# A feed-forward layer's last six chunks: the up-projection as a block product of seven, with its weight sums made on the way

## The chip, the cores and the metric

The kernel runs on one core of a Trainium2 chip. The core has a matrix engine (TensorE, PE in the profile; its weight loads are PEld), a vector engine (VectorE, DVE), an activation engine (ScalarE, ACT), a general engine (GpSimd, POOL) and a queue engine that here only issues transfers (SyncE, SP). Each engine runs its own instructions in order and waits on semaphores for the others. SBUF is the on-chip memory of 128 partitions; PSUM holds the results of matmuls. The metric is the device time of one launch in microseconds; the median of three runs is compared.

## The reference

An attention layer with a window feeds a gated feed-forward layer (FFN). In short:

```python
batch, n_heads, seq, head_dim = (8, 8, 576, 64)
scores = scale * np.matmul(q, k.transpose(0, 1, 3, 2))
mask = (rel >= 0) & (rel < window)                    # window 128
scores = np.where(mask, scores + bias[None], -1000000000.0)
attn = np.exp(scores - max); attn = attn / (sum + 1e-09)
attn_out = np.matmul(attn, v)
x = attn_out.transpose(0, 2, 1, 3).reshape(4608, 512)
h = x @ w_in                                          # 512 -> 2048
g = h * (1.0 / (1.0 + np.exp(-1.702 * h)))
out = g @ w_out                                       # 2048 -> 512
```

All of it is float32. The matmuls run in a shorter float format (fp32r), so every large operand is cut in a high part and a rest, and a product of two operands is made of three: high by high, rest by high, high by rest.

## The kernel before

**FFN.** The 4608 tokens are 18 chunks of 256. `Job` walks the 16 blocks of 128 hidden features of one chunk; a block of a chunk is a step, 288 in all. A step's *up* (L552) is 12 matmuls of 128x256 into `h_ps`: three products (`xh` by both parts of `w`, `xl` by the high part) over four slices of the 512 inputs. Then ACT makes tanh (L557), DVE the gelu product `g` (L558, which reads PSUM), ACT casts `g` to `gh` (L561), and POOL makes the rest `gl = g - gh` (L562). The step's *down* (L571) is 6 matmuls of 128x512 into the two accumulators of the chunk. Up of the next step is issued before down of this one. At a chunk's start `split_x` cuts `x` (casts L536 on DVE or ACT, subtractions L538 on DVE and POOL by turns); at its end DVE scales the accumulators into `o` (L587) and ACT's queue writes them out.

**Weights.** `w_in` and `w_out` come as 16 + 16 blocks of 512 KB over SP's queue and are decoded at the start: L212 and L213 on DVE, casts on ACT, the rest on POOL (L217). All 32 stay in SBUF, under the tags `w1_0` to `w1_15` and `w2_0` to `w2_15`.

**Attention.** It is cut in units, one for a pair of heads and one or two blocks of 128 queries. A call of `tick()` moves a pipeline of units by one stage: cuts of q, k, v (L292 to L312), scores (L334), bias and minimum (L362), exponentials (L381), normalising (L406), transposes (L442), the cut of the transposed probabilities (L461), the product with v (L499), and the sums into `x` (L520 to L529). There are 144 units; the first two batches have a simpler path without cuts.

**What sets the order.** The program interleaves FFN steps and ticks. `due` says for each batch how many units must be done by which chunk and from which chunk on they may start; the loop spreads the ticks by that. A scheduler then orders the instructions of each engine; queues are in order after that. `in_turn` adds dependencies between matmuls to keep their order. `XBUFS = 4` buffers hold chunks of `x` that attention has begun.

Of the kernel before, what the change touches and what calls it, by code (L numbers as in the profile page):

```python
# [8 lines left out]
F32 = mybir.dt.float32  # L9
F32R = mybir.dt.float32r  # L10
# [14 lines left out]
NF = DFF // P  # L25
NC = DM // P
T = 256
NCH = NT // T
XBUFS = 4
WINDOW = 128  # L30
MASKED = -1.0e38
SCALE = 0.125
# [4 lines left out]
WB = 2  # L37
# [105 lines left out]
def tile_kernel(ctx: ExitStack, tc: tile.TileContext, q0, k0, v0, qT, kT, v, w_in, w_out, out):  # L143
    nc = tc.nc

    const = ctx.enter_context(tc.tile_pool(name="const", bufs=1))
    raw = ctx.enter_context(tc.tile_pool(name="raw", bufs=3))
    att = ctx.enter_context(tc.tile_pool(name="att", bufs=2))
    xp = ctx.enter_context(tc.tile_pool(name="xp", bufs=1))
    ffn = ctx.enter_context(tc.tile_pool(name="ffn", bufs=2))  # L150
    ps = ctx.enter_context(tc.tile_pool(name="ps", bufs=1, space=PSUM))

    def move(dst, src):

# [333 lines left out]
    def mix(u):  # L488
# [4 lines left out]
        for c in u.chunks:  # L493
# [22 lines left out]
    def sum_up(u, g):
        hp = u.pair % NP
# [14 lines left out]
    def split_x(c, x):  # L532
        xh = xp.tile([P, NC, T], F32R, name="xh")
        xl = xp.tile([P, NC, T], F32R, name="xl")
        for k in range(NC):
            (nc.scalar.copy if c in BESIDE else nc.vector.tensor_copy)(xh[:, k], x[:, k])  # L536
            sub = nc.vector if k % 2 else nc.gpsimd
            sub.tensor_tensor(xl[:, k], x[:, k], xh[:, k].bitcast(F32), ALU.subtract)  # L538
        return xh, xl

    class Job:


        def __init__(self, c, f0, f1, begun=None):
            self.c, self.f0, self.f1, self.begun = c, f0, f1, begun
            self.gs = {}

        def up(self, f):
            h = ps.tile([P, T], F32, name="h_ps", bufs=2)
            ops = [(z, x, k) for z, x in ((0, self.xh), (1, self.xh), (0, self.xl)) for k in range(NC)]  # L550
            for n, (z, x, k) in enumerate(ops):
                nc.tensor.matmul(  # L552
                    h, w1[f][:, z, k * P:(k + 1) * P], x[:, k],
                    start=(n == 0), stop=(n == len(ops) - 1))

            g = ffn.tile([P, T], F32, name="g")
            nc.scalar.activation(g, h, AF.Tanh, scale=0.851)  # L557
            nc.vector.scalar_tensor_tensor(g, g, 1.0, h, ALU.add, ALU.mult)  # L558
            gh = ffn.tile([P, T], F32R, name="gh")
            gl = ffn.tile([P, T], F32R, name="gl")  # L560
            nc.scalar.copy(gh, g)  # L561
            nc.gpsimd.tensor_tensor(gl, g, gh.bitcast(F32), ALU.subtract)  # L562
            self.gs[f] = (gh, gl)

        def down(self, f):
            if f == self.f0:
                self.acc = [ps.tile([P, DM], F32, name=f"acc{t}") for t in range(T // P)]
            gh, gl = self.gs.pop(f)
            for n, (g, z) in enumerate(((gh, 0), (gh, 1), (gl, 0))):
                for t, acc in enumerate(self.acc):  # L570
                    nc.tensor.matmul(  # L571
                        acc, g[:, t * P:(t + 1) * P], w2[f][:, z],
                        start=(f == self.f0 and n == 0), stop=(f == self.f1 - 1 and n == 2))

        def finish(self):
            if self.f1 < NF:
                self.sum = xp.tile([P, T // P, DM], F32, name="xf", tag="xf", bufs=XBUFS)
# [3 lines left out]
            o = xp.tile([P, T // P, DM], F32, name="o", tag="x0")  # L581
            for t, acc in enumerate(self.acc):
                if self.begun:
                    nc.vector.tensor_tensor(o[:, t], acc, self.begun.sum[:, t], ALU.add)
                    nc.vector.tensor_scalar(o[:, t], o[:, t], 0.5, None, ALU.mult)
                else:
                    nc.vector.tensor_scalar(o[:, t], acc, 0.5, None, ALU.mult)  # L587
                at = self.c * T + t * P
                nc.scalar.dma_start(out[at:at + P, :], o[:, t])
# [17 lines left out]
    ticks = 0  # L607

    def tick():

        nonlocal ticks
        n = ticks

        def stage(k, *steps):
            u = units[n + k] if 0 <= n + k < len(units) else None
            for step in steps:
                if u:
                    step(u)

        stage(1, split_q)  # L620
        stage(-2, flip, split_v)
        stage(0, load_v)
        stage(-1, biased)
        stage(1, split_rest)
        stage(-1, exponents)
        stage(-1, normal)
        stage(-2, high, low)
        stage(0, scores)
        stage(-3, mix)
        if n + 1 < len(units) and units[n + 1] and loads:  # L630
# [38 lines left out]

    jobs = [Job(0, 0, F0), Job(1, 0, NF)]  # L670
    jobs.append(Job(0, F0, NF, jobs[0]))
    jobs += [Job(c, 0, NF) for c in range(2, NCH)]
# [10 lines left out]
    def begin(j):  # L683
        j.xh, j.xl = split_x(j.c, xf.pop(j.c, first_x))
        j.up(j.f0)

    begin(jobs[0])
    seen = 0
    flat = [(j, f) for j in jobs for f in range(j.f0, j.f1)]
    for now, (j, f) in enumerate(flat):  # L690

        if halves < 2 * NF:
            owed += max(
                (2 * g + 2 - halves - owed) / max(need[g] - DECODE_AHEAD - now, 1)
                for g in range(halves // 2, NF))
            while owed >= 1 and halves < 2 * NF:
                owed -= 1
                fetch_upto(halves // 2 + 1 + FETCH_AHEAD)
                decode_next()

        pace, last = 0.0, 0
        for n, by, start in due:
            if start > seen:
                break
            last = n + 3
            pace = max(pace, (n + 3 - ticks - credit) / max(starts[by] - 1 - SLACK - now, 1))
        credit += pace
        while credit >= 1 and ticks < last:
            credit -= 1
            tick()  # L710
        if now + 1 < len(flat):
            nj, nf = flat[now + 1]
            if nj is j:
                j.up(nf)
            else:
                begin(nj)
                seen = max(seen, nj.c)
        j.down(f)
        if f == j.f1 - 1:
            j.finish()  # L720


def build(nc, arrays):
# [50 lines left out]
```

## Time and profile before

| | |
|---|---|
| median of 3 runs | 1065.19 us (1064.08 to 1066.76) |
| profiled execution | 1068.36 us, span 1066.3 us, granted clock 0.995 |
| PE busy | 1052.9 us, 99% of the span |
| DVE, ACT, POOL busy | 660.5, 597.2, 603.5 us (62, 56, 57%) |
| up matmuls, L552 | 3456 of 128x256 |
| down matmuls, L571 | 1728 of 128x512 |
| transfers | 78.45 MB, mean 74 GB/s |

The page lists busy time by engine, the span in forty slices, the chain of waits that ended last, and groups of instructions. Other views used below are stretches (busy time of each engine between two times), one line's instructions, the chain in order of time, and the timeline. A line number such as L552 is that of the kernel before; the change's own lines are numbered by the changed kernel.

### The profile page before, as it was taken

What the parts mean: (1) busy time and instruction counts of PE and PEld (TensorE: products, weight loads), DVE (VectorE), ACT (ScalarE), POOL (GpSimd) and SP (SyncE); (2) the same over time, 40 slices, a digit from 0 to 9 for tenths busy, and PEclk for the clock granted to TensorE, in tenths of its full rate; (3) what the DMA queues carried; (4) which work ended last, traced back from release to release, by engine and by line L of the source; (5) the groups of instructions that cost most, each with busy time, mean ns of one, the idle gap of its engine ahead of it and who ended that gap; (6) DMA issues with size and microseconds to landing.
All of it is one profiled execution on the core that took longest, in us unless ns stands there. A gap on an engine that the chain in (4) does not pass through costs nothing.

```text
span 1066.3 us, 21362 instructions
## 1 busy us (share of the span) xinstructions
PE 1052.9 (99%) x7041; PEld 929.1 (87%) x7041; DVE 660.5 (62%) x2117; ACT 597.2 (56%) x1811; POOL 603.5 (57%) x863
## 2 busy tenths in 40 slices
PE   9899999999999999999999999999999999999998
PEld 5567787889989999999999999999999999998987
DVE  6797522568887777545767668767877687313121
ACT  6879853466666565535555556655665656322222
POOL 4579933567676666554656557656666665323232
PEclk9899999999999999999999999999999999999999
DMA  8872001223222132102121223212222221000000
GB/s 307 281 261 73 25 22 56 73 67 96 75 76 81 51 102 67 57 14 71 54 79 52 71 62 91 66 60 78 79 63 85 57 78 28 20 2 20 1 21 20
DMA packets 88109, 78.45 MB, mean 74 GB/s; under 512 B 36800, under 2 KB 79296, under 8 KB 88000
## 3 DMA queue, kind: packets, MB, share of 16 engines
q1 hardware_dynamic: 82240, 67.14, 21.4%
q10 hardware_dynamic: 5760, 9.96, 2.6%
q8 instruction: 55, 0.90, 0.3%
q14 instruction: 54, 0.44, 0.1%
HBM read 67.63 MB, written 9.44 MB: 72 GB/s over the span
## 4 chain that ended last, share of the span: by engine, by line
PE 94%; DVE 3%; ACT 1%; DMA 1%; issue 1%; POOL 0%; SPq 0%; DVEq 0%; POOLq 0%; ACTq 0%
PE h_ps L552 38%; PE acc L571 37%; PE s_ps L334 5%; PE x_ps L499 5%; PE t_ps L442 4%; PE x_ps L476 2%; PE t_ps L419 1%; PE sb_ps L324 1%; PE s_ps L324 1%; DVE wc L213 1%; DMA rw<-w_out 1%; ACT pb L374 1%; DVE rec L392 0%; PE acc L189 0%; DVE rw L212 0%
## 5 line engine op out<-in xcount | busy, mean ns | idle before, releaser
L562 POOL TENSOR_TENSOR gl<-g,gh 128x256 fp32r<-128x256 f32 x288 | 218.0, 757 | 292.2 <-ACT gh L561 224.9
L552 PE MATMUL h_ps<-xh,w 128*128 128x256 f32 x2304 | 370.2, 284 | 1.1 <-POOL w L217 0.6
L552 PEld LDWEIGHTS h_ps<-xh,w 128*128 128x128 f32 x2304 | 328.5, 189 | 34.5 <-issue 2.8
L571 PE MATMUL acc<-w,gh 128*128 128x512 f32 x1152 | 324.9, 400 | 0.0
L558 DVE SCALAR_TENSOR_TENSOR g<-g,h_ps 128x256 f32<-128x256 f32 x288 | 119.6, 415 | 207.9 <-ACT g L557 206.5
L557 ACT ACTIVATE g<-h_ps 128x256 f32<-128x256 f32 x288 | 110.4, 383 | 229.4 <-PE h_ps L552 207.3
L571 PEld LDWEIGHTS acc<-w,gh 128*128 128x128 f32 x1152 | 196.5, 189 | 27.9 <-ACT g L557 0.3
L552 PE MATMUL h_ps<-xl,w 128*128 128x256 f32 x1152 | 194.6, 280 | 0.0
L561 ACT CAST gh<-g 128x256 fp32r<-128x256 f32 x288 | 116.9, 406 | 129.5 <-DVE g L558 121.1
L571 PE MATMUL acc<-w,gl 128*128 128x512 f32 x576 | 188.0, 401 | 0.0
L552 PEld LDWEIGHTS h_ps<-xl,w 128*128 128x128 f32 x1152 | 164.2, 188 | 6.0
L312 POOL TENSOR_TENSOR K<-rk,K 128x384 fp32r<-128x384 f32 (+1 forms) x120 | 109.0, 909 | 65.2 <-ACT Q L292 15.9
L381 ACT ACTIVATE pb<-pb,mins 128x256 f32<-128x256 f32 (+2 forms) x216 | 104.9, 487 | 43.8 <-DVE mins L362 40.1
L571 PEld LDWEIGHTS acc<-w,gl 128*128 128x128 f32 x576 | 92.6, 188 | 9.5 <-issue 0.9
L311 POOL TENSOR_TENSOR Q<-rq,Q 64x256 fp32r<-64x256 f32 (+1 forms) x120 | 83.1, 692 | 22.2 <-DVE K L310 4.9
L406 DVE TENSOR_SCALAR pb<-pb,rec 128x256 f32<-128x256 f32 (+2 forms) x216 | 91.8, 461 | 3.2
L362 DVE CUSTOM_DVE_ANT_0 pb<-s_ps,bias 128x256 f32<-128x256 f32 (+3 forms) x240 | 85.7, 377 | 4.1 <-PE s_ps L334 2.8
L392 DVE TENSOR_SCALAR rec<-sums 128x2 f32<-128x2 f32 (+3 forms) x144 | 48.5, 336 | 58.4 <-ACT pb L381 53.6
L334 PE MATMUL s_ps<-K,Q 128*128 128x256 f32 (+1 forms) x432 | 79.8, 289 | 0.4 <-DVE mins L362 0.4
L310 DVE CAST K<-rk 128x384 fp32r<-128x384 f32 (+1 forms) x120 | 52.5, 438 | 41.2 <-PE s_ps L334 34.2
L461 DVE TENSOR_TENSOR pl<-t_ps,ph 128x512 fp32r<-128x512 f32 (+2 forms) x120 | 72.2, 604 | 9.3 <-ACT ph L455 6.6
L442 PE MATMUL t_ps<-ident,pb 128*128 128x128 f32 x408 | 74.2, 272 | 0.0
(68 smaller groups left out, 1322.2 us busy)
## 6 DMA issues: line engine op xcount, KB each, us to landing
rk<-kT SPq DMA_DIRECT2D x72, 192.0 KB, 2.5
rq<-qT SPq DMA_DIRECT2D x96, 128.0 KB, 2.3
out<-o ACTq DMA_DIRECT2D x36, 256.0 KB, 2.1
rw<-w_in SPq DMA_DIRECT2D x16, 512.0 KB, 6.5
rw<-w_out SPq DMA_DIRECT2D x16, 512.0 KB, 7.0
rk<-kT SPq DMA_DIRECT2D x48, 128.0 KB, 2.2
rv<-v SPq DMA_DIRECT2D x96, 64.0 KB, 1.9
rq<-q SPq DMA_DIRECT2D x16, 128.0 KB, 2.6
```

What stands on the lines that cost most here:

```text
L312: nc.gpsimd.tensor_tensor(K2, rk, K1.bitcast(F32), ALU.subtract)
L334: nc.tensor.matmul(u.s[:b.rows, e, b.first:b.end], u.Q[:, b.q0 - u.q0:b.q0 - u.q0 + b.rows], k[:, ko:ko + b.end - b.first], start=(z == 0) ...
L362: nc.vector.tensor_tensor_reduce(b.p[ra:rb, cs:b.end], u.s[ra:rb, e, cs:b.end], bias[head][ra:rb, cs:b.end], -SCALE, BIG, ALU.add, ALU.min ...
L381: nc.scalar.activation(live, live, AF.Exp, bias=u.mins[:b.rows, e:e + 1], scale=-1.0, accum_out=u.sums[:b.rows, e:e + 1],)
L406: nc.vector.tensor_scalar(live, live, u.rec[:rows, e:e + 1], None, ALU.mult)
L442: nc.tensor.transpose(u.t[:c.n, w:w + b.rows], b.p[:b.rows, col:col + c.n], ident[:b.rows, :b.rows])
L552: nc.tensor.matmul(h, w1[f][:, z, k * P:(k + 1) * P], x[:, k], start=(n == 0), stop=(n == len(ops) - 1))
L557: nc.scalar.activation(g, h, AF.Tanh, scale=0.851)
L558: nc.vector.scalar_tensor_tensor(g, g, 1.0, h, ALU.add, ALU.mult)
L561: nc.scalar.copy(gh, g)
L562: nc.gpsimd.tensor_tensor(gl, g, gh.bitcast(F32), ALU.subtract)
L571: nc.tensor.matmul(acc, g[:, t * P:(t + 1) * P], w2[f][:, z], start=(f == self.f0 and n == 0), stop=(f == self.f1 - 1 and n == 2))
```

## The change

The classical way, a step at a time, stays for chunks 0 to 11 (`S0 = 12`). The last six chunks are taken in three pairs. For a pair, the 512 inputs are halved, the two chunks are the two columns, and two feature blocks are the two rows of a 2x2 block product in Winograd's form of Strassen's scheme: seven products in place of eight. Block `j` of eight covers features `2j` and `2j + 1`. Each product is 6 matmuls of 128x256 (two slices of inputs, three part products). The first two, B11 and B21, belong to the plain operands; X and Y are two PSUM buffers in which sums grow over several products, and copies by ACT and additions by DVE make the four results from them. The weight operands are A11, A12, A22 and four sums S1 to S4; the token operands are B11, B21, B22 and four combinations T1 to T4.

The weight sums are made by `sums(j)` in the last 20 classical steps (`SUMS`), one block every two steps: six DVE operations on SBUF, then for two pairs of sums a cast by ACT, a subtraction by POOL. All seven operands, cut in two parts, go to DRAM (`part`) over SP's queue, and `factor` reads them back in a ring of five buffers of 512 KB, two operands a buffer; the buffers are those of the first weight matrix, which is needed no more. `Pair.split` cuts the seven token operands. `linked` pins TensorE's order through the whole block product: each product is followed by a `cover` of downs of the block before. The last two classical downs (`COVER = 2`) are kept for the first pair's start.

So that the last steps are free of attention, batches 2 to 7 may all start once chunk 2 is begun, and all attention is due 20 steps before the block product. Chunks of `x` that are done too early are sent to DRAM (`send`) and recalled one chunk ahead (`recall`). `XBUFS` becomes 5; `o` uses the buffers of another pool.

```diff
-XBUFS = 4
+XBUFS = 5
+S0 = 12
+T2 = 2 * T
+COLS = 2 * P
+RING = 5
+SUMS = 20
+COVER = 2
+ORDER = "A11", "A12", "S2", "S3", "S1", "S4", "A22"
+OPERANDS = "B11", "B21", "T2", "T3", "T1", "B22", "T4"
...
+    def send(ct):
+        away[ct] = dram.tile([P, NC, T], F32, name=f"x{ct}")
+        nc.sync.dma_start(away[ct], xf.pop(ct))
+    def recall(ct):
+        if ct in away:
+            nc.sync.dma_start(home(ct), away.pop(ct))
...
+    def sums(j):
+        f, g = w1[2 * j], w1[2 * j + 1]
+        for name, src in (("A11", f[:, :, :COLS]), ("A12", f[:, :, COLS:]), ("A22", g[:, :, COLS:])):
+            nc.sync.dma_start(part(j, name), src.bitcast(F32))
+        a = att.tile([P, 2 * COLS], F32, name="sa", tag="ph")
+        b = att.tile([P, 2 * COLS], F32, name="sb", tag="pl")
+        nc.vector.tensor_tensor(a, g[:, 0].bitcast(F32), g[:, 1].bitcast(F32), ALU.add)
+        nc.vector.tensor_tensor(b, f[:, 0].bitcast(F32), f[:, 1].bitcast(F32), ALU.add)
+        nc.vector.tensor_tensor(a[:, COLS:], a[:, :COLS], a[:, COLS:], ALU.add)
+        nc.vector.tensor_tensor(a[:, :COLS], b[:, :COLS], a[:, :COLS], ALU.subtract)
+        nc.vector.tensor_tensor(b[:, :COLS], a[:, COLS:], b[:, :COLS], ALU.subtract)
+        nc.vector.tensor_tensor(b[:, COLS:], b[:, COLS:], b[:, :COLS], ALU.subtract)
+        for s, names in ((a, ("S3", "S1")), (b, ("S2", "S4"))):
+            st = xp.tile([P, 2, 2 * COLS], F32R, name="st", tag="xf", bufs=XBUFS)
+            nc.scalar.copy(st[:, 0], s)
+            nc.gpsimd.tensor_tensor(st[:, 1], s, st[:, 0].bitcast(F32), ALU.subtract)
+            for i, name in enumerate(names):
+                nc.sync.dma_start(part(j, name), st[:, :, i * COLS:(i + 1) * COLS].bitcast(F32))
...
+    def factor(n):
+        at, side = divmod(n, 2)
+        while len(ring) < min(at + RING, (NCH - S0) // 2 * len(parts)):
+            r = const.tile([P, 2, 2, COLS], F32R, name="ring", tag=f"w1_{len(OPERANDS) + len(ring) % RING}")
+            nc.sync.dma_start(r.bitcast(F32), parts[len(ring) % len(parts)])
...
+        def product(self, j, n, bank, start):
+            w, x = factor(self.first + j * len(ORDER) + n), self.x[OPERANDS[n]]
+            ops = [(z, y, k) for z, y in ((0, 0), (1, 0), (0, 1)) for k in range(2)]
+            linked([
+                nc.tensor.matmul(
+                    bank, w[:, z, k * P:(k + 1) * P], x[:, y, k],
+                    start=start and i == 0, stop=i == len(ops) - 1, skip_group_check=True)
+                for i, (z, y, k) in enumerate(ops)])
...
     units, due = [], []
     for b in range(B):
-        start = max((b * S + S - 1) // T - XBUFS, 0)
         if b < WB:
...
-                due.append((len(units), (b * S + lo) // T, start))
+                due.append((len(units), (b * S + lo) // T, 0))
         else:
             units += whole_batch(b)
-            due.append((len(units), b * S // T, start))
+            due.append((len(units), b * S // T, WB))
...
+    for c in range(S0, NCH):
+        starts[c] = steps - SUMS
...
+        if made < NF // 2 and now >= len(flat) - SUMS + 2 * made:
+            sums(made)
+            made += 1
```

**TensorE in the last chunks.** Before, around the start of the last chunk; `h_ps` is an up, `acc` a down:

```order
L552 MATMUL h_ps<-xh,w_1_525 128x256 x3
L552 MATMUL h_ps<-xl,w_1_525 128x256 x4
L552 MATMUL h_ps<-xh,w_2_573 128x256 x8
L552 MATMUL h_ps<-xl,w_2_573 128x256 x4
L571 MATMUL acc_14643<-w_0_455,gh 128x512 x2
L571 MATMUL acc_14643<-w_0_455,gl 128x512
```

After, from the second block to the third of the first pair; `X_ps` and `Y_ps` take products (`xB`, `xT` are token operands, `ring` the weight operands), `accs` are downs with `gs`:

```order
L693 MATMUL X_ps<-xB_13093,ring 128x256 x6
L693 MATMUL Y_ps<-xB_13096,ring 128x256 x6
L752 MATMUL accs<-w_0_485,gs 128x512 x6
L693 MATMUL X_ps<-xT_13105,ring 128x256 x6
L752 MATMUL accs<-w_0_485,gs 128x512 x6
L693 MATMUL Y_ps<-xT_13108,ring 128x256 x6
L693 MATMUL X_ps<-xT_13111,ring 128x256 x6
L752 MATMUL accs<-w_1_592,gs 128x512 x6
L693 MATMUL X_ps<-xB_13100,ring 128x256 x6
L693 MATMUL Y_ps<-xT_13115,ring 128x256 x6
L752 MATMUL accs<-w_1_592,gs 128x512 x6
```

Seven products of six and four groups of six downs make a block of two features for two chunks. At the very start of the first pair there are only two groups of late classical downs between the first products, and the others stand one behind the other.

**VectorE in the last classical steps.** Before, in steps 178 to 180, the operations of attention stand between the gelu products (L558):

```order
L558 SCALAR_TENSOR_TENSOR g<-g,h_ps 128x256
L310 CAST K_10795<-rk 128x384
L362 ISA pb,mins<-s_ps,bias_75 128x256
L362 ISA mins 128x1
L526 TENSOR_TENSOR carry<-x_ps,xb 64x128
L529 TENSOR_TENSOR xf<-x_ps,xb 64x128
L529 TENSOR_TENSOR xf<-x_ps,xb 64x256
L461 TENSOR_TENSOR pl<-t_ps,ph 128x512
```

After, there is no attention left; between the gelu products (L576) stand the sums (L626 to L631) and the first pair's token operands (L675 to L686):

```order
L576 SCALAR_TENSOR_TENSOR g<-g,h_ps 128x256
L631 TENSOR_TENSOR sb<-sb 128x256
L626 TENSOR_TENSOR sa<-w_9_1113 128x512
L628 TENSOR_TENSOR sa<-sa 128x256
L679 TENSOR_TENSOR xf<-xf 128x512
L576 SCALAR_TENSOR_TENSOR g<-g,h_ps 128x256
L681 TENSOR_TENSOR xf<-xf 128x512
L627 TENSOR_TENSOR sb<-w_8_1043 128x512
L629 TENSOR_TENSOR sa<-sb,sa 128x256
```

The sums of all eight blocks lie between the gelu products of steps 174 and 187; the 16 subtractions that belong to them (L635) lie in POOL's order among the `gl` of the same steps.

**SyncE at the start.** Before, the loads of early units and weights follow one another:

```order
L155 DMA VV<-v 128x3x128
L155 DMA rq<-q 128x64
L155 DMA rk<-k 128x192
L155 DMA rw_5_379<-w_in 128x512
L155 DMA rw_5_381<-w_out 128x512
```

After, at the same place:

```order
L164 DMA VV<-v 128x3x128
L623 DMA part_84<-w_0_417 128x2x256 x2
L164 DMA rq<-q 128x64
L164 DMA rk<-k 128x192
L164 DMA rw_5_409<-w_in 128x512
L164 DMA rw_5_411<-w_out 128x512
```

The two stores of decoded weights (A11 and A12 of block 0) wait for the decoding of that weight; 22 more such stores stand between the later loads of weights.

More of the change, by code (lines that the diff above doesn't have):

```diff
@@ L151, in tile_kernel @@
     ps = ctx.enter_context(tc.tile_pool(name="ps", bufs=1, space=PSUM))
+    dram = ctx.enter_context(tc.tile_pool(name="dram", bufs=1, space=bass.MemoryType.DRAM))
     def move(dst, src):
@@ L568, in down @@
             gh, gl = self.gs.pop(f)
+            products = []
             for n, (g, z) in enumerate(((gh, 0), (gh, 1), (gl, 0))):
                 for t, acc in enumerate(self.acc):
-                    nc.tensor.matmul(
+                    products.append(nc.tensor.matmul(
                         acc, g[:, t * P:(t + 1) * P], w2[f][:, z],
-                        start=(f == self.f0 and n == 0), stop=(f == self.f1 - 1 and n == 2))
+                        start=(f == self.f0 and n == 0), stop=(f == self.f1 - 1 and n == 2)))
+            return products
         def finish(self):
             if self.f1 < NF:
-                self.sum = xp.tile([P, T // P, DM], F32, name="xf", tag="xf", bufs=XBUFS)
+                self.sum = xp.tile([P, T // P, DM], F32, name="sum", tag="xf", bufs=XBUFS)
                 for t, acc in enumerate(self.acc):
@@ L586, in finish, with part @@
                 else:
-                    nc.vector.tensor_scalar(o[:, t], acc, 0.5, None, ALU.mult)
+                    nc.vector.tensor_scalar(o, acc, 0.5, None, ALU.mult)
                 at = self.c * T + t * P
-                nc.scalar.dma_start(out[at:at + P, :], o[:, t])
+                nc.scalar.dma_start(out[at:at + P, :], o)
+    parts = [dram.tile([P, 2, 2, COLS], F32, name=f"part{i}") for i in range(NF // 2 * len(ORDER) // 2)]
+    def part(j, name):
+        at, side = divmod(j * len(ORDER) + ORDER.index(name), 2)
+        return parts[at][:, side]
@@ new lines, in tile_kernel, with linked @@
+    ring = []
+    def factor(n):
[3 more added lines that the diff above has]
+            nc.sync.dma_start(r.bitcast(F32), parts[len(ring) % len(parts)])
+            ring.append(r)
+        return ring[at][:, side]
+    chain = []
+    def linked(products):
+        in_turn(chain + products)
+        chain[:] = products[-1:]
@@ L606, in tile_kernel @@
     loads = [u for u in units if u]
-    ticks = 0
+    ticks, seen = 0, 0
     def tick():
@@ L631, in tick @@
             load(loads.pop(0))
+        for ct in full.get(n - 3, ()):
+            if ct > seen + 1:
+                send(ct)
         ticks += 1
@@ L671, in tile_kernel @@
     jobs.append(Job(0, F0, NF, jobs[0]))
-    jobs += [Job(c, 0, NF) for c in range(2, NCH)]
+    jobs += [Job(c, 0, NF) for c in range(2, S0)]
     starts = {}
@@ L683, in begin, with advance @@
     def begin(j):
+        nonlocal seen
+        recall(j.c)
         j.xh, j.xl = split_x(j.c, xf.pop(j.c, first_x))
+        seen = max(seen, j.c)
+        recall(seen + 1)
+        if seen == S0 - 1:
+            recall(S0 + 1)
         j.up(j.f0)
[L687 to L699, printed above, removed]
+    def advance(now):
+        nonlocal credit
         pace, last = 0.0, 0
@@ L710, in tile_kernel @@
             tick()
+    begin(jobs[0])
+    made = 0
+    flat = [(j, f) for j in jobs for f in range(j.f0, j.f1)]
+    late = []
+    for now, (j, f) in enumerate(flat):
+        if halves < 2 * NF:
+            owed += max(
+                (2 * g + 2 - halves - owed) / max(need[g] - DECODE_AHEAD - now, 1)
+                for g in range(halves // 2, NF))
+            while owed >= 1 and halves < 2 * NF:
+                owed -= 1
+                fetch_upto(halves // 2 + 1 + FETCH_AHEAD)
+                decode_next()
+        advance(now)
+        if made < NF // 2 and now >= len(flat) - SUMS + 2 * made:
+            sums(made)
+            made += 1
         if now + 1 < len(flat):
@@ L716, in tile_kernel, with cover @@
                 begin(nj)
[L717 to L720, printed above, removed]
+        if now < len(flat) - COVER:
+            j.down(f)
+            if f == j.f1 - 1:
+                j.finish()
+        else:
+            late.append(f)
+    assert made == NF // 2 and ticks >= due[-1][0] + 3
+    before = None
+    for c in range(S0, NCH, 2):
+        pair = Pair(c)
+        pair.split()
+        for ct in (c + 2, c + 3):
+            recall(ct)
+        for i in range(NF // 2 * 4):
+            if before is None and i < 4:
+                def cover():
+                    if i < len(late):
+                        linked(j.down(late[i]))
+                        if i == len(late) - 1:
+                            j.finish()
+            elif i < 4:
+                cover = lambda: before.down(NF // 2 - 1, i)
+            else:
+                cover = lambda: pair.down(i // 4 - 1, i % 4)
+            pair.up(i // 4, i % 4, cover)
+        before = pair
+    for q in range(4):
+        before.down(NF // 2 - 1, q)
 def build(nc, arrays):
```

110 lines of the change are left out of this document (102 added, 8 removed).

## Prediction

> **What bounds the kernel now.** I read first the busy shares and the chain of waits on the page, then busy time by stretches, then the chain in order of time near the end.
>
> ```profile
> PE 1052.9 (99%) x7041; PEld 929.1 (87%) x7041; DVE 660.5 (62%) x2117; ACT 597.2 (56%) x1811; POOL 603.5 (57%) x863
> PE 94%; DVE 3%; ACT 1%; DMA 1%; issue 1%; POOL 0%; SPq 0%; DVEq 0%; POOLq 0%; ACTq 0%
> ```
>
> TensorE (PE) is busy for 99% of the span and makes 94% of the chain. So a matmul that goes away is worth its spacing, as long as no other engine becomes the later one. The spacing stands in the chain near the end:
>
> ```profile
> 1056.30 1.40 PE h_ps L552 x12
> 1046.51 1.40 PE acc L571 x6
> 1061.71 0.69 DVE o L587
> ```
>
> The columns are start, length, engine, tile. Twelve up matmuls of 128x256 take 1.40 us, 0.117 each; six down matmuls of 128x512 take 1.40, 0.233 each. A step (one feature block of one chunk) is 2.80 us. Next, how near the other engines are:
>
> ```profile
> 316.00:918.00 602.00, 601.94 (x4130) 553.79 (x4129) 419.01 (x1395) 341.72 (x1043) 362.46 (x557) 1.00 0.23 65
> 316.00:918.00 602.00, 304.92 (x2064) 282.64 (x2064) 1.00 0.23 65
> 960.00:1000.00 40.00, 40.00 (x257) 36.08 (x256) 10.32 (x22) 11.21 (x29) 11.97 (x16) 1.00 0.04 14
> 240.00:320.00 80.00, 79.57 (x559) 73.19 (x558) 68.14 (x224) 53.36 (x165) 56.89 (x89) 1.00 0.29 83
> 75.00:90.00 15.00, 13.94 (x91) 9.66 (x91) 14.93 (x37) 14.57 (x48) 13.04 (x13) 1.00 0.44 146
> ```
>
> Each row has the stretch, its length, then busy us of PE, weight load, DVE, ACT, POOL (with instruction counts), the granted clock, the DMA share and GB/s. The second row is line L552 alone: 2064/12 = 172 steps. In the long stretch PE is full, DVE is at 0.70 and POOL at 0.60. In the last chunks, without attention, DVE drops to 0.26 and POOL to 0.30. The two last rows are the densest stretches: DVE 0.85 beside a PE that lost 0.43 of 80 us, and DVE 1.00 with POOL 0.87 beside a PE that lost 1.06 of 15.
>
> **The saving.** A pair of chunks costs 16 x 2 x 12 = 384 up matmuls now, and 8 x 7 x 6 = 336 after; the downs stay. 48 x 0.117 = 5.6 us for a pair, **16.8 us** for three. The Trainium skill (TensorE: Matmul & The Clock Gate, "Wait — 56ns, not 53.3ns?") gives N/2.4 GHz plus 2.5 ns between warm matmuls, 109 ns here; the saving would be 15.7 us. The chain's 117 ns differs from it, at a granted clock of 1.00, so the measured spacing stands in the sum.
>
> **Denser attention.** The new table of due times ends attention at step 172 where it ended near 236. Worked through, the table gives 100 ticks in the steps from 64 to 236 before, 97 ticks in the steps from 64 to 168 after: 0.58 a step becomes 0.93. A tick's work follows from the long stretch less its FFN. DVE: a step without attention has 10.32 x 2.80/40 = 0.72 us, so 419 - 172 x 0.72 = 295 us for 100 ticks, 2.95 each. POOL: (362 - 172 x 0.84)/100 = 2.2. PE: (602 - 172 x 2.80)/100 = 1.2. A step after then has PE 2.80 + 0.93 x 1.2 = 3.92, DVE 0.72 + 2.74 = 3.46 (0.88 of PE), POOL 0.84 + 2.05 = 2.89 (0.74). The stage takes 104 x 3.92 = 408 us of PE. The nearest rows bound its stalls: 0.43 of 80 gives 2.2 us; 1.06 of 15 gives 29. By the order one chunk of the eight (steps 112 to 128, where outputs, x cuts and attention pile up) holds about 62 us of DVE for 63 of PE; I give that chunk the dear rate, 4.4, and the other 345 us the cheap one, 1.9: **+6.3 us**.
>
> **The weight sums.** These eight blocks stand in DVE's order between the gelu products of steps 174 and 187: 13 steps, 36.4 us of PE. Prices come from these rows:
>
> ```profile
> L538 DVE TENSOR_TENSOR xl<-xf,xh x34: 409/900/1523, 88.2 to 1015.6; 128x256 fp32r<-128x256 f32 x34
> L538 POOL TENSOR_TENSOR xl<-xf,xh x34: 727/787/1190, 89.7 to 1014.3; 128x256 fp32r<-128x256 f32 x34
> L217 POOL TENSOR_TENSOR w<-wc,w x32: 1266/1288/2787, 21.4 to 131.4; 128x512 fp32r<-128x512 f32 x32
> 50.35 0.68 DVE L213 SCALAR_TENSOR_TENSOR wc<-wc,rw 128x512 int32<-128x512 int32 x1
> 53.50 0.93 POOL L402 TENSOR_SCALAR pb<-pb,rec 64x192 f32<-64x192 f32 x1
> 53.73 2.51 DVE L213 SCALAR_TENSOR_TENSOR wc<-wc,rw 128x512 int32<-128x512 int32 x1
> 54.41 1.28 POOL L217 TENSOR_TENSOR w<-wc,w 128x512 fp32r<-128x512 f32 x1
> L558 DVE SCALAR_TENSOR_TENSOR g<-g,h_ps 128x256 f32<-128x256 f32 x288 | 119.6, 415 | 207.9 <-ACT g L557 206.5
> L562 POOL TENSOR_TENSOR gl<-g,gh 128x256 fp32r<-128x256 f32 x288 | 218.0, 757 | 292.2 <-ACT gh L561 224.9
> ```
>
> In the first three, three numbers are shortest, median and longest ns. DVE in these 13 steps: 23 operations of 128x512 on SBUF alone (16 of the sums, 7 for the pair's x) at 0.68 are 15.6; 34 of 128x256 at 0.41 are 13.9; 13 gelu products at 0.415 are 5.4; casts, outputs and residues of attention about 3.9: 38.8 us, already above PE's 36.4. POOL: 16 differences of the sums and 4 of x at 1.27 are 25.4; 12 of gl at 0.74 are 8.9; 2 of xl are 1.5: 35.8 us, 0.98 of PE. Worse, the two don't run side by side: the subtraction L538 takes DVE 0.41 us at its shortest and 0.90 in the median, and the 2.51 us L213 above covers a POOL operation that ends at 54.43 and another that ends at 55.69, and itself ends 0.55 us later. The gelu product reads PSUM and keeps its 0.415.
>
> The gelu product on DVE and gl on POOL stand behind the sums in their queues, and PE's down matmuls wait for both. From below, the price is the densest row's rate, 1.06 of 15: 2.6 us in 36.4. From above: if DVE's SBUF operations (31.2 us) and all of POOL's (35.8) exclude each other, they need 67.0 us, 30.6 more than PE. In the densest row DVE was full with waits counted in; here it is over full without them. So the price lies well above the lower end; about halfway, **+15 us**. The Trainium skill (SBUF — State Buffer, "SBUF: two separate sides") says that the pair of ports that DVE and GpSimd share is an exclusive lock: a DVE operation with two SBUF inputs and a GpSimd operation block each other for their whole length. By it the upper end would be the price; the 2.51 us row agrees with it, no row shows how much of a long crowd PE can hide.
>
> **Into the block product.** PE's order then has seven products without enough downs between them (the late ones cover two). A product into X waits for ACT's copy of the one before, and the next gelu for DVE. The tail shows such steps:
>
> ```profile
> 1056.35 0.42 DVE L558 SCALAR_TENSOR_TENSOR g<-g,h_ps 128x256 f32<-128x256 f32 x1 [1.91 <-ACT g L557]
> 1056.80 0.41 ACT L561 CAST gh<-g 128x256 fp32r<-128x256 f32 x1 [0.49 <-DVE g L558]
> ```
>
> Each hand-over is some 0.5 us beyond a product of six (0.70): from one to ten of these, 1 to 5 us, taken **+3**. Later, every block (10.5 us: 42 x 0.117 + 24 x 0.233) has a down of 1.40 us behind each hand-over, and DVE needs about 2.8 us, POOL 2.5 of the 10.5. These cost nothing; without the downs they would cost the 0.5 each.
>
> **Transfers.** Each pair re-reads 28 tiles of 512 KB in 84 us, 175 GB/s.
>
> ```profile
> GB/s 307 281 261 73 25 22 56 73 67 96 75 76 81 51 102 67 57 14 71 54 79 52 71 62 91 66 60 78 79 63 85 57 78 28 20 2 20 1 21 20
> rw<-w_in SPq DMA_DIRECT2D x16, 512.0 KB, 6.5
> rw<-w_out SPq DMA_DIRECT2D x16, 512.0 KB, 7.0
> ```
>
> The first slice moved 307 GB/s; a tile lasts 10.5/3.5 = 3.0 us, a refill has four tiles, 12 us, against a landing of 7.0. Hidden; if a landing doubled to 14, PE would wait 2 of every 3 us for as long as it lasted. Twelve chunks of x go out and come back (512 KB each way, the return issued a chunk ahead, some 60 us), in slices that move 14 to 102 GB/s: nothing, or with a return at 7.0 us on the path, 7.0 each. SP's order also has the 24 stores of weights (256 KB each, 6.3 MB) among the first loads: the first two stand ahead of rq, rk and rw_5, each behind POOL's decode. 0.5 MB at 307 GB/s is 1.7 us, all 24 are 20; since the following 512 KB loads are wanted later than that, 0 to 4, taken **+1**. At the end four accumulators, not two, go out through DVE and ACT: one output more at 0.69, **+0.5**.
>
> **Sum.** -16.8 + 6.3 + 15 + 3 + 1 + 0.5 = +9.0. The profiled execution took 1068.36 us (span 1066.3), which is 3.2 above the median of the runs, 1065.19. So 1077.4 on the profiled one, and **1074** as a median.
>
> **Rivals.**
> *Gain kept.* The lower ends hold: -16.8 + 2.2 + 2.6 + 1 = -11, **1054**. For it: in the densest row DVE and POOL together counted 28.0 busy us in 15 and PE lost only 7%. Against it: that row is 15 us long, and its 28.0 has the waits for each other in it; here 67.0 in 36.4 comes before any wait. It decides if PE's share in steps 174 to 187 stays above 0.9.
> *Full exclusion in the sums.* +30.6 for 15: +24.6, **1090**. For it: the 2.51 us row. Against: the sums of one block may slip behind later steps, since the last is wanted some 70 us on. It decides where DVE's rows of L626 to L631 last twice their 0.68 and 0.41. The skill's rule named above is this rival.
> *DVE bounds the dense stage.* 29 for 6.3 over 408 us: +31.7, **1097**. For it: 0.88 is above the 0.85 of the densest long stretch; DVE's operations lengthen further beside a fuller POOL. Against: at 0.85 PE lost only 0.5%.
> *The block product starves.* If the ring's loads land late, 2 us a tile in the first pair alone is +56; a few tiles, +8, **1082**.
>
> **Chances.** Forecast 0.42, its own range 1066 to 1084; gain kept 0.37, 1052 to 1067; full exclusion 0.11; dense stage 0.06; starving 0.04. No change is within 0.3%, 3.2 us, about what a measurement of this kernel can tell: 1062 to 1068.4. It takes 0.08 of the forecast and 0.06 of the kept gain. So faster 0.31, same 0.14, slower 0.34 + 0.21 = 0.55. The range 1054 to 1094 leaves out about 0.1 at each end.
>
> **What would show it.** Right: PE's busy time in the last 260 us near 84 us a pair; in steps 174 to 187 some 50 us for 36.4 of work, with PE idle behind gl and g, DVE's sums well above 0.68; in the stage before, PE above 0.97. Wrong: PE full through the sums (then 1054 to 1060); PE idle before the block product's matmuls, on a DMA; a later start of the second step of weights, with rw behind the stores; or PE losing 5% all through the dense stage.

## The result and the profile after

The changed kernel takes 1092.92 us (median of four runs, 1092.7 to 1093.07) against 1065.54 for the kernel before in the same comparison: a ratio of 1.0257, 95% interval 1.024 to 1.0275. It is 27 us slower; the forecast was 9 us slower. In the page of the changed kernel, busy time by engine and the chain by engine:

```profile
PE 1053.8 (97%) x6897; PEld 920.1 (84%) x6897; DVE 770.6 (71%) x2192; ACT 632.2 (58%) x1854; POOL 627.2 (57%) x831
PE 40%; DVE 8%; issue 2%; ACT 1%; POOL 0%; DMA 0%; POOLq 0%; ACTq 0%; DVEq 0%
```

The 144 matmuls saved are there (7041 before, 6897 now), and PE's busy time is no shorter for it; DVE has 110 us more, and 8% of the chain where it had 3%. (The chain as shown covers about half of this span.) Three stretches of the changed kernel: attention at its densest, the weight sums, and the block product with its entry. Columns as before: stretch, length, then PE, PEld, DVE, ACT, POOL busy, granted clock, DMA share, GB/s.

```profile
316.00:740.00 424.00, 413.82 (x2830) 374.96 (x2829) 374.08 (x1234) 277.50 (x870) 298.35 (x467) 1.00 0.35 101
762.00:819.00 57.00, 45.32 (x255) 39.19 (x254) 55.77 (x77) 21.75 (x49) 41.55 (x35) 0.91 0.61 203
829.00:1091.00 262.00, 255.82 (x1584) 229.12 (x1582) 113.61 (x167) 99.91 (x214) 74.88 (x57) 1.00 0.53 174
```

The first stretch in the kernel before:

```profile
316.00:740.00 424.00, 424.00 (x2908) 390.18 (x2907) 290.52 (x966) 238.01 (x727) 254.38 (x389) 1.00 0.23 66
```

In the same 424 us the changed kernel issues 78 matmuls fewer; DVE is at 0.88 where it was at 0.69. In the sums DVE is busy for 55.8 of 57 us, and PE idles for 11.7 of them.

To see where the time went I take the start of each step's gelu product from the trace, less 2.80 us a step and 1.2 us for each tick done by then (counted by DVE's reciprocals). What remains is a lag that grows where PE loses time. Within a chunk it swings by 2 to 3 us in both kernels (before: 79.2 at step 158, 82.1 at step 159), so smaller differences are not read.

| lag in us at step | 64 | 96 | 128 | 160 | 174 | 187 | 191 |
|---|---|---|---|---|---|---|---|
| before | 80.9 | 80.1 | 81.8 | 82.1 | 79.9 | 79.4 | 83.2 |
| after | 78.0 | 87.1 | 97.7 | 100.7 | 102.1 | 122.6 | 121.7 |

So the start is 2.9 us shorter, the dense stage (64 to 174) loses 24.1 where before it gained 1.0, the sums lose 19.6 by step 191 where before the lag moved by 3.3. That is -2.9 + 25.1 + 16.3 = 38.5 us. From step 191 to the end the changed kernel takes 1091.2 - 829.3 = 261.9 us; before it was 1066.3 - 757.2 = 309.1, of which 28 ticks of attention are 33.6: 13.6 us less, the 16.8 saved and 3.2 for entry and end. 38.5 - 13.6 = 24.9 us, the difference of the spans.

A second count, also from the trace, needs no price of a tick: from the start of each matmul to the start of the next, less the mean of its kind in the kernel before between 316 and 900 us (117 ns for an up and 233 for a down from step 172 on). By it the changed kernel loses 24.9 us in steps 64 to 174, 18.4 from step 172 to 191, and after that 1.3 more than the kernel before loses there.

**The sums.** A piece of the chain in order of time (start, length, engine, tile), and PE's longest wait from 760 to 820 us (total, times, longest):

```profile
775.91 1.36 DVE sa L626
777.27 0.88 DVE sa L629
778.21 0.73 issue
778.94 1.78 DVE sb L627
780.72 0.33 DVE sb L630
781.05 1.71 DVE xB L675
782.77 0.34 DVE sa L629
783.10 0.33 DVE g L576
```

```profile
PE h_ps L570 <- DVE g L576: 11.5, 6, 3.8
```

DVE's queue is the path. The gelu product, 0.33 us of the chain, stands behind operations whose shortest is 0.68 or 0.41 and that now take up to 1.78, and PE waits for it. DVE's 76 operations of steps 174 to 187 would take 37.5 us at the shortest length of each line and shape in this trace, little more than PE's 36.4; they filled nearly all of 57.

**The start of a chunk.** In the dense stage the losses sit around the starts of chunks: by the second count 23.3 of the 24.9 us lie between the last two steps of a chunk and the fourth of the next. All that PE is shown to wait for from 320 to 600 us is DVE's; the largest of it:

```profile
PE s_ps L343 <- DVE mins L371: 2.2, 3, 1.1
PE h_ps L570 <- DVE g L576: 1.5, 2, 1.0
PE h_ps L570 <- DVE xh L554: 1.3, 4, 0.4
```

The start of step 112, from the timeline:

```profile
503.58 1.76 DVE L554 CAST xh<-xf 128x256 fp32r<-128x256 f32 x3
503.61 0.84 POOL L580 TENSOR_TENSOR gl<-g,gh 128x256 fp32r<-128x256 f32 x1
504.41 0.77 POOL L556 TENSOR_TENSOR xl<-xf,xh 128x256 fp32r<-128x256 f32 x1
504.65 0.38 PE L570 MATMUL h_ps<-xh,w 128*128 128x256 f32 x1 [0.35 <-DVE xh L554]
505.33 0.27 DVE L554 CAST xh<-xf 128x256 fp32r<-128x256 f32 x1
505.39 0.39 PE L570 MATMUL h_ps<-xh,w 128*128 128x256 f32 x1 [0.24 <-DVE xh L554]
```

Three casts of DVE last 1.76 us beside two operations of POOL, where the fourth lasts 0.27, and PE gets one slice of `x` at a time.

### The profile page after: what moved, and what is told of

Read it like the earlier page. It is cut to its first block, busy times and chain, and to the rows that moved or that the text cites. A ratio compares the mean times of both kernels' runs of the same rounds, so it can differ in the third digit from the quotient of the medians.

```text
span 1091.2 us, 21571 instructions
## 1 busy us (share of the span) xinstructions
PE 1053.8 (97%) x6897; PEld 920.1 (84%) x6897; DVE 770.6 (71%) x2192; ACT 632.2 (58%) x1854; POOL 627.2 (57%) x831
## 4 chain that ended last, share of the span: by engine, by line
PE 40%; DVE 8%; issue 2%; ACT 1%; POOL 0%; DMA 0%; POOLq 0%; ACTq 0%; DVEq 0%
PE accs L752 11%; PE acc L590 8%; PE h_ps L570 6%; PE X_ps L693 6%; PE Y_ps L693 4%; PE s_ps L343 2%; PE x_ps L508 2%; PE t_ps L451 1%; DVE pb L415 1%; DVE sb L627 1%; DVE sa L626 1%; DVE pl L470 1%; DVE pb L371 1%; ACT pb L390 1%; DVE xh L554 0%
## 5 line engine op out<-in xcount | busy, mean ns | idle before, releaser
L570 PE MATMUL h_ps<-xh,w 128*128 128x256 f32 x1536 | 254.7, 290 | 15.6 <-DVE g L576 13.7
L570 PEld LDWEIGHTS h_ps<-xh,w 128*128 128x128 f32 x1536 | 218.5, 192 | 38.9 <-DVE g L576 17.4
L590 PE MATMUL acc<-w,gh 128*128 128x512 f32 x768 | 228.5, 406 | 0.4 <-DVE o L607 0.4
L580 POOL TENSOR_TENSOR gl<-g,gh 128x256 fp32r<-128x256 f32 x192 | 149.5, 781 | 109.2 <-ACT gh L579 70.9
L705 POOL TENSOR_TENSOR gs<-g,gs 128x512 fp32r<-128x512 f32 x48 | 63.4, 1321 | 168.7 <-PE Y_ps L693 120.4
L590 PEld LDWEIGHTS acc<-w,gh 128*128 128x128 f32 x768 | 132.6, 190 | 21.4 <-DVE o L607 0.9
L752 PE MATMUL accs<-w,gs 128*128 128x512 f32 x576 | 148.4, 393 | 0.3 <-POOL gs L705 0.3
L570 PE MATMUL h_ps<-xl,w 128*128 128x256 f32 x768 | 139.2, 287 | 0.1
L590 PE MATMUL acc<-w,gl 128*128 128x512 f32 x384 | 129.9, 408 | 2.1 <-POOL gl L580 2.1
L752 PEld LDWEIGHTS accs<-w,gs 128*128 128x128 f32 x576 | 102.2, 189 | 17.7 <-POOL gs L705 0.7
L576 DVE SCALAR_TENSOR_TENSOR g<-g,h_ps 128x256 f32<-128x256 f32 x192 | 79.1, 413 | 48.5 <-ACT g L575 47.7
L575 ACT ACTIVATE g<-h_ps 128x256 f32<-128x256 f32 x192 | 73.2, 383 | 64.1 <-PE h_ps L570 55.8
```

Source lines behind the costliest of these rows:

```text
L570: nc.tensor.matmul(h, w1[f][:, z, k * P:(k + 1) * P], x[:, k], start=(n == 0), stop=(n == len(ops) - 1))
L590: products.append(nc.tensor.matmul(acc, g[:, t * P:(t + 1) * P], w2[f][:, z], start=(f == self.f0 and n == 0), stop=(f == self.f1 - 1 and ...
L752: products.append(nc.tensor.matmul(self.acc[t], g[:, y, t * P:(t + 1) * P], w2[f][:, z], start=(f == 0 and n == 0), stop=(f == NF - 1 and ...
```

## The experiments

Theory A: DVE's operations that have only SBUF operands and those of POOL exclude each other, so in the crowd DVE falls behind, and PE waits for it. Rival B: it is DVE's own work and the order of its queue. Rival C: buffers wait for transfers to and from DRAM.

**e1: the denser attention alone.** No sums, no block product.

```diff
-    jobs += [Job(c, 0, NF) for c in range(2, S0)]
+    jobs += [Job(c, 0, NF) for c in range(2, NCH)]
...
-        if made < NF // 2 and now >= len(flat) - SUMS + 2 * made:
-            sums(made)
-            made += 1
```

> All 18 chunks the classical way, with the change's table of due times, its five x buffers and its spills; no weight sums, no block product. Counted in the trace of the changed kernel, the steps from 64 to 174 take 24 us more than their matmuls and ticks did before, and the start is 2 us shorter. Theory A (the crowd of attention on DVE and POOL is the cost): 1065.5 + 22 = 1087, with the same 24 us between steps 64 and 174. Rival C (the cost comes from the stores of weights at the start, or from what the sums add to the queues): under 1072.

Measured: 1084.91 us, ratio 1.0186 (1.0159 to 1.0212), 19 us above before. Its lag goes from 78.9 at step 64 to 101.3 at 174, and stands at 100.7 at 187. The dense stage costs its 22 us without any sum or block product near it.

**e2: POOL's part of the sums left out.**

```diff
-            nc.gpsimd.tensor_tensor(st[:, 1], s, st[:, 0].bitcast(F32), ALU.subtract)
+            nc.scalar.copy(st[:, 1], s)
```

> In the weight sums the rests are left wrong: ACT writes a second copy of the sum (16 x 0.6 us) where POOL subtracted (16 x 1.27 us), so the outputs of the last six chunks are off; all else stays. The sums stage lost 20 us. Theory A (DVE's operations with SBUF inputs and POOL's exclude each other): their sum falls from 67 to 47 us for 36.4 of PE, the loss to about 10, the time to 1083. Rival B (DVE's own work, 38.8 us for 36.4, and the order of its queue): the loss stays, 1091 to 1093. Rival C (the buffers of the sums wait for their stores to DRAM): stays, 1093.

Measured: 1086.56 us, 1.0201 (1.0175 to 1.0226), 6.4 less than the changed kernel. From step 174 to 187 the lag grows by 13.5 instead of 20.5. That is between the theories: A had expected 10 less. Without POOL's subtractions the same additions are back near their shortest length, shortest/median/longest ns (in the changed kernel this line has 680/1054/1790):

```profile
L627 DVE TENSOR_TENSOR sb<-w x8: 676/684/1223, 760.7 to 798.1; 128x512 f32<-128x512 f32 x8
```

That is the exclusion seen directly; but two thirds of the loss stayed. The added copies got in the way; from 750 to 830 us DVE's largest wait is for ACT:

```profile
DVE g L576 <- ACT g L575: 21.7, 11, 4.1
```

where in the changed kernel the same wait sums to 11.4. How much of the 13.5 is these copies and how much is DVE's own queue is not told apart.

**e3: DVE's additions left out.**

```diff
-        nc.vector.tensor_tensor(a, g[:, 0].bitcast(F32), g[:, 1].bitcast(F32), ALU.add)
-        nc.vector.tensor_tensor(b, f[:, 0].bitcast(F32), f[:, 1].bitcast(F32), ALU.add)
...
+        nc.scalar.copy(a, g[:, 0].bitcast(F32))
+        nc.scalar.copy(b, f[:, 0].bitcast(F32))
```

> The six DVE operations of each weight sum are left out; ACT copies a plain weight in their place (16 x 0.6 us), so the outputs of the last six chunks are off. POOL's subtractions and the stores stay. DVE falls from 38.8 to 14 us in the sums stage. Theory A: DVE and POOL together 42 us for 36.4, the loss falls from 20 to about 5, the time to 1078. Rival B: the loss is gone, 1073. Rival C (stores): it stays, 1093.

Measured: 1075.38 us, 1.0098 (1.0075 to 1.0121), 17.5 less than the changed kernel. The lag grows by 5.2 from 174 to 187, as A had it; the time lies midway between A's 1078 and B's 1073, so this run alone does not decide between them. C is out for the sums: the stores to DRAM are all still there. In 762 to 812 us of this run PE is full, and POOL has become the fullest of the others:

```profile
762.00:812.00 50.00, 49.29 (x311) 43.17 (x311) 20.30 (x34) 33.48 (x73) 42.30 (x40) 1.00 0.84 288
```

**e4: the casts of x on ACT.**

```diff
-            (nc.scalar.copy if c in BESIDE else nc.vector.tensor_copy)(xh[:, k], x[:, k])
+            nc.scalar.copy(xh[:, k], x[:, k])
```

> The four casts of x at each chunk's start go to ACT in all classical chunks, where DVE makes them from chunk 4 on in the changed kernel. In its trace the dense stage loses its time in the 20 us around each chunk's start, where the casts take DVE up to 2.2 us beside POOL. Theory A: the loss of eight starts, some 2 to 3 us each, falls by about half: 8 to 12 us less, 1081 to 1085. Rival (the recall of x from DRAM is late, or the loss is spread over the whole stage by density): no change, within 2 us of 1093.

Measured: 1088.37 us, 1.0219 (1.0194 to 1.0243), 4.5 less. The dense stage's lag grows by 18.9 instead of 24.1. By the second count that stage loses 16.3 instead of 24.9, within what was expected of the casts, but the sums lose 2 us more, and the whole gain is about half of that.

**e5: the sums through PSUM.** A copy by ACT opens each sum in PSUM; every DVE operation of the sums then has one operand in PSUM and one in SBUF. The rests of S1 and S2 go from POOL to DVE, those of S3 and S4 stay on POOL.

```diff
+        nc.scalar.copy(pa, g[:, 0].bitcast(F32))
+        nc.vector.tensor_tensor(pa, pa, g[:, 1].bitcast(F32), ALU.add)
+        nc.scalar.copy(pb, f[:, 0].bitcast(F32))
+        nc.vector.tensor_tensor(b, pb, f[:, 1].bitcast(F32), ALU.add)
+        nc.scalar.copy(a[:, hi], pa[:, hi])
+        nc.vector.tensor_tensor(pa[:, hi], pa[:, lo], a[:, hi], ALU.add)
+        nc.vector.tensor_tensor(a[:, lo], b[:, lo], pa[:, lo], ALU.subtract)
+        nc.vector.tensor_tensor(pb[:, lo], pa[:, hi], b[:, lo], ALU.subtract)
+        nc.vector.tensor_tensor(b[:, hi], b[:, hi], pb[:, lo], ALU.subtract)
...
+                on = nc.vector if name in ("S1", "S2") else nc.gpsimd
+                on.tensor_tensor(st[:, 1, cs], src, st[:, 0, cs].bitcast(F32), ALU.subtract)
```

> The sums' intermediate results stand in PSUM (two banks that attention no longer uses), so that every DVE operation of the sums has at most one SBUF input; ACT makes four more copies a block (two of 512, one of 256 more, four casts of 256 for two of 512); the rests of S1 and S2 go from POOL to DVE, those of S3 and S4 stay on POOL. DVE's work in the stage grows from 38.8 to 45 us, POOL's falls from 35.8 to 27. Theory A (exclusion between SBUF operations): what still excludes itself is POOL's 27 and 7 of DVE's, 34 us, under 36.4, so the loss of 20 falls to 5 to 9, the time to 1078 to 1082. Rival B (DVE's own fill): DVE has more to do, the loss grows to 25 or so, 1097. Rival C (the buffers of the sums wait for their stores): stays, 1093.

Measured: 1075.5 us, 1.0092 (1.0073 to 1.011), 17.4 less than the changed kernel. The lag grows by 1.7 from 174 to 187: the loss in the sums is gone, though DVE has more to do (45 us for 38.8, by the count made ahead of the run). What two of the sums' lines last, shortest/median/longest ns, in the changed kernel:

```profile
L627 DVE TENSOR_TENSOR sb<-w x8: 680/1054/1790, 761.5 to 813.6; 128x512 f32<-128x512 f32 x8
L629 DVE TENSOR_TENSOR sa<-sb,sa x8: 412/902/1399, 767.4 to 814.3; 128x256 f32<-128x256 f32 x8
```

and in e5:

```profile
L632 DVE TENSOR_TENSOR sb<-sb,w x8: 681/684/692, 765.6 to 806.3; 128x512 f32<-128x512 f32 x8
L635 DVE TENSOR_TENSOR sa<-sb,pa x8: 405/421/422, 766.3 to 807.6; 128x256 f32<-128x256 f32 x8
751.00:809.00 58.00, 58.00 (x380) 52.64 (x379) 47.63 (x108) 40.22 (x107) 35.34 (x44) 1.00 0.68 232
```

The same additions, with one operand in PSUM, last their shortest time every time, with POOL at work beside them. DVE is at 0.82 and PE loses nothing. Two things else moved. POOL has half of the rests, 16 of 128x256 for 16 of 128x512; but e2, with none of them on POOL, still lost 13.5. And these sums spread wider: the first addition stands at 751.6 us, the others from 764 to 810, some 16 steps, where the crowd of the changed kernel stood in 13. So the run shows that the operations are no longer lengthened and that the loss is gone with it; how much the wider spread did is not told apart.

**e6: half of the normalising on ACT, beside the casts.**

```diff
-            nc.vector.tensor_scalar(live, live, u.rec[:rows, e:e + 1], None, ALU.mult)
+            if e:
+                nc.scalar.activation(live, live, AF.Copy, scale=u.rec[:rows, e:e + 1])
+            else:
+                nc.vector.tensor_scalar(live, live, u.rec[:rows, e:e + 1], None, ALU.mult)
```

> Beside the casts of x, every second normalising multiplication of attention (SBUF to SBUF) goes from DVE to ACT, half of 216. DVE loses some 0.35 us and ACT gains 0.5 us a tick. Theory A: the dense stage, DVE 0.88 of it, falls to 0.78, and its loss from 24 us (19 with the casts moved) to 8 or less: 1075 to 1079. Rival (ACT, at 0.66 of the stage, becomes the late one, with 0.78): the loss stays near 19, 1088. Rival (the stage's loss is in the order of the queues, whatever they hold): 1086 to 1090.

Measured: 1076.05 us, 1.0099 (1.0074 to 1.0124). The dense stage's lag grows by 8.6; that of the sums still by 21.7.

**e7: both, the diffs of e5 and e6.**

> e5 and e6 in one kernel. Theory A: the two losses are at different places and add, 44 us become some 15: 1062 to 1068, about the kernel before. Rival (they are one loss, moved on): no better than the better of the two.

Measured: 1058.41 us, 0.9928 (0.9909 to 0.9948). The two losses are at two places and add: 17.4 and 16.9 apart, 34.5 together. This one is faster than the kernel before.

**e8: the same relief of DVE in the kernel before.** The diffs of e4 and e6, on the kernel before.

> The kernel before with the edits of e6 alone. Its DVE is at 0.70 while attention runs and its PE loses under 3 us in 600. Theory A: no gain where DVE is not late, 1063 to 1067. Rival (these edits are worth the same anywhere): 15 us less, 1050.

Measured: 1065.44 us, 0.9998 (0.9987 to 1.0009). Its page:

```profile
PE 1050.9 (99%) x7041; PEld 928.0 (87%) x7041; DVE 609.0 (57%) x1965; ACT 654.4 (61%) x1963; POOL 601.8 (56%) x863
```

DVE has 51 us less to do and the time is the same. DVE was no bound before; the change made it one.

**e9: POOL's rest of K left out.** This takes POOL's work from the dense stage and leaves DVE's queue as it is.

```diff
-        nc.gpsimd.tensor_tensor(K2, rk, K1.bitcast(F32), ALU.subtract)
+        nc.scalar.copy(K2, rk)
```

> The changed kernel with POOL's largest work for attention left out: the rest of K (120 subtractions of 0.9 us) is a second copy by ACT (0.5 us), so scores and all outputs are off. DVE's instructions and their order stay as they are. The dense stage lost 25 us. Theory A (the exclusion of DVE's and POOL's SBUF operations makes it): POOL goes from 0.70 to some 0.55 of the stage, the loss to 12 or less, the time to 1080 or less. Rival (DVE's own fill of 0.88 and the order of its queue): the loss stays at 22 to 25, 1090 to 1093. Rival (ACT becomes late, at 0.80): it grows.

Measured: 1084.39 us, 1.0185 (1.0161 to 1.0209), 8.5 less than the changed kernel. The dense stage's lag grows by 15.6 instead of 24.1, between A's 12 and B's 22.

```profile
316.00:740.00 424.00, 418.63 (x2907) 382.46 (x2905) 364.04 (x1272) 317.59 (x990) 220.38 (x383) 1.00 0.35 101
```

POOL is at 0.52, DVE still at 0.86, now for more matmuls in the same time. So POOL's work beside DVE's carries some 8 us of the dense loss, with DVE's queue as it was; the rest stays with a DVE that is nearly full, and with the part of POOL's work that is still there. This run does not tell these two apart.

**e10 and e11: from e7 on.** e10 puts the sums later, e11 moves the cast of K to ACT.

```diff
-SUMS = 20
+SUMS = 14
...
-        if made < NF // 2 and now >= len(flat) - SUMS + 2 * made:
+        if made < NF // 2 and now >= len(flat) - SUMS + 3 * made // 2:
```

> The kernel of e7 with the sums in the last 14 classical steps, three blocks in four steps or so, and attention due six steps later: 97 ticks in 110 steps, 0.88 a step for 0.93. Theory A: of the 10 us that the dense stage of e7 still loses some 3 go, the sums stage stays free: 1055 to 1058. Rival (the sums, at 4.4 us of DVE each, no longer fit): the loss goes to them, 1060 to 1066.

```diff
-        nc.vector.tensor_copy(K1, rk)
+        nc.scalar.copy(K1, rk)
```

> The kernel of e7 with the cast of K (120 of 0.44 us) on ACT too. Theory A: DVE's SBUF work falls by another 10% of the stage, the dense loss of 10 us to about 5: 1053 to 1056. Rival (ACT, at 0.77 of the stage and then 0.86, is the next one late): no gain or a loss, 1058 to 1066.

Measured: e10 1053.93 us, 0.9898 (0.9879 to 0.9917); e11 1051.55 us, 0.987 (0.9848 to 0.9892). Both gained more than was expected. In e11 the dense stage's lag no longer grows (79.1 to 78.2):

```profile
316.00:740.00 424.00, 423.97 (x2992) 392.13 (x2991) 317.20 (x1106) 362.70 (x1116) 303.46 (x486) 1.00 0.37 108
```

DVE is at 0.75, ACT at 0.86, and PE is full with 162 matmuls more than the changed kernel issued in this stretch. POOL does as much as it did there. Beside e9's row, DVE and POOL together are busy for 621 us here and for 584 there, yet it is e9 that loses 15 us. What differs is DVE's own share, 0.75 here and 0.86 there. So as far as these two rows go, DVE's own queue carries the larger part of the dense loss, and the crowding with POOL the smaller.

**e12: both of these.**

> e10 and e11 together: the casts of K on ACT and the sums in the last 14 steps. e11 stands at 1051.6, e10 at 1053.9, e7 at 1058.4. Theory A (both relieve the same crowd of the dense stage, of which little is left): 1049 to 1052, most of it e11's. Rival (they add): 1047. The sum without any stall is 1065 - 16.8 + 3 = 1051, less the 3 us by which the start is earlier, 1048.

Measured: 1050.74 us, 0.9864 (0.9848 to 0.9881): 14.4 us under the kernel before and 42 under the changed one. That is inside A, and only 0.8 less than e11 alone, which is within the spread of e11's runs (1050.77 to 1052.92).

```profile
PE 1033.2 (98%) x6897; PEld 911.4 (87%) x6897; DVE 657.6 (63%) x1960; ACT 730.5 (70%) x2142; POOL 607.4 (58%) x831
PE 90%; DMA 3%; DVE 2%; ACT 2%; POOL 1%; issue 1%; SPq 0%; POOLq 0%; ACTq 0%
```

PE's busy time is now some 20 us below that of the kernel before, and the chain is PE's again.

## Why the prediction was right and wrong

The direction held. The time lay just inside the outer range (1054 to 1094) and outside the forecast's own (1066 to 1084); the size was three times the forecast. By the terms of its sum:

- *Saving, entry and end: -16.8 + 3 + 0.5.* Right, as near as the trace tells: from step 191 on it has 13.6 us less, 3.2 of the 16.8 lost; by the second count 1.3 are lost. The entry in the chain shows what was priced, hand-overs of half a microsecond between the first products:

```profile
832.12 0.57 issue
832.69 0.69 DVE o L607
833.79 0.38 ACT u L728
834.21 0.99 PE X_ps L693 x6
835.23 0.39 ACT g L699
835.64 0.43 DVE g L700
```

- *Transfers: 0, and +1 for the stores at the start.* The ring never made PE wait; its 512 KB land in 3.3 us, half of the bound that was used:

```profile
ring<-part SPq DMA_DIRECT2D x84, 512.0 KB, 3.3
```

The start got 2.9 us shorter instead. e1, without those stores, starts 2.0 shorter; what shortens it I didn't isolate.

- *Sums: +15, with bounds 2.6 and 30.6.* Right in place and mechanism, and nearly in size: 16 to 21 by the lag, 18.4 by the second count. The size was in part luck: the point halfway was chosen, no row set it, and up to 5 us of what came may be the clock's (last section), for which the sum had no term. e3 and e5 moved the loss as the exclusion of DVE and POOL says, e2 by 7 of the 10 that were expected. The Trainium skill (SBUF — State Buffer, "SBUF: two separate sides") puts this down to a pair of ports that a DVE operation with two SBUF inputs and a GpSimd operation that reads SBUF lock against each other; the traces agree, 0.68 to 1.79 us with two SBUF inputs, 0.68 to 0.69 with one. By it, and by the prediction's own estimate, the full 30.6 would have been lost. The prediction's 67.0 us of DVE's and POOL's SBUF work passed in 57, so some 10 us of it ran side by side; which part could, no run here shows.

- *Dense attention: +6.3, with bounds 2.2 and 29.* This is the step that failed. It gave the dear rate (1.06 us in 15) to one chunk, steps 112 to 128, and the cheap one (0.43 in 80, read from a row with DVE at 0.85) to the other 345 us, whose average was to be 0.88. The trace has 24.1: 9.1 from step 64 to 96, 10.6 from 96 to 128, 4.4 from there to 174. By the second count the chunk that starts at step 112 lost 7.8 where 4.4 was priced, and the other six 17.1 where 1.9 was. The loss does not follow the average. At a chunk's start four casts, four subtractions and two outputs join DVE's and POOL's queues at once, and with attention at 0.91 ticks a step (steps 64 to 128) there is too little slack in which that crowd can drain. At 0.83 (128 to 174) the loss is a third of that, in the kernel before, at 0.55 over steps 64 to 174, it is nothing. e6 and e11, which take work from DVE and none from POOL, bring it to 8.6 and to nothing; so what the price left out is DVE's queue at those starts. The rival *DVE bounds the dense stage* had this mechanism, at 29 us a chance of 0.06, and it is what came, beside the forecast's own sums.

- *Rivals.* *Gain kept* failed at both stages. *Full exclusion in the sums* came in kind and not in size: 16 to 21 for 30.6. *The block product starves* did not happen. The two dear rivals moved one term each and left the other at the forecast; the sums came somewhat above their price and the dense stage near its upper bound. Both hang on DVE's time, so their chances were not independent.

- *What would show it.* The signs for the sums came: 56.9 us for 36.4 of work, PE idle behind `g`, additions up to 1.79 us. The prediction also looked for PE above 0.97 before the sums: it was 413.82 of 424, 0.976, and that alone would have passed as right while over 20 us went. A share of busy time hides such losses, since each matmul's busy time is longer than its spacing (an up has 290 ns in the page's mean and follows the one before it by 117); the lag by steps shows them.

## What to carry to other kernels

Before work is moved into fewer steps, sum for each engine what each step then holds, and look at the starts of chunks first: a stage whose bursts find no slack there loses at each of them, while the average is still below full. Where VectorE and GpSimd both work from SBUF, do not price VectorE's operations at their shortest (here 0.68 us became up to 1.79). If a crowd of such operations can't be moved in time, give each VectorE operation one operand in PSUM, or move plain casts and scalings to ScalarE: here the two together turned a loss of 27 us into a gain of 13 (e11), and the move to ScalarE was worth nothing in the kernel where VectorE had slack (e8). And judge stages by how fast steps pass, not by the busy share of the bound engine.

## What the hardware showed beside

The clock that TensorE is granted fell after some idle times inside the sums, and so an idle time could cost more than its length. In the changed kernel's trace the clock has two values, 1.00 and 0.50. Three stretches of 3.41 us at 0.50 lie in the sums, from 775.05, 798.95 and 805.77 us, and one in the dense stage, from 375.69. Two of PE's idle times, and then the inside of the four stretches:

```profile
771.00:774.00 3.00, 0.00 (x0) 0.00 (x0) 3.00 (x8) 2.21 (x5) 1.85 (x2) 1.00 0.89 274
795.00:798.00 3.00, 0.18 (x1) 0.00 (x0) 3.00 (x4) 0.00 (x1) 1.82 (x2) 1.00 1.03 310
775.10:778.40 3.30, 3.30 (x14) 2.91 (x13) 3.30 (x5) 1.84 (x4) 3.30 (x3) 0.50 1.07 384
799.00:802.30 3.30, 3.30 (x13) 3.11 (x14) 3.30 (x3) 1.81 (x4) 3.15 (x3) 0.50 0.36 128
805.80:809.10 3.30, 3.30 (x15) 3.11 (x14) 3.23 (x5) 1.47 (x4) 3.01 (x3) 0.50 0.00 0
375.70:379.10 3.40, 3.40 (x16) 3.40 (x17) 3.20 (x13) 1.56 (x6) 2.42 (x5) 0.50 0.22 57
```

The idle times just before the three in the sums are 3.4, 3.8 and 1.9 us long, the one before 375.69 is 1.0; an idle time of 1.8 us that ended at 783.49 had no such stretch behind it. Over the 57 us of the sums the clock averaged 0.91, about 5 us of matmul time. The forecast had no term for it. DVE was full in the same rows, so how much of the 5 us lengthened the kernel is not shown. In the rows of e3 and e5 above, where PE hardly idled, the clock stayed at 1.00.
